# Full 128-column products in place of pairs of 64-column halves in a retention and MLP kernel

## The chip, the cores and the metric

The kernel runs on one core of one Trainium2 chip. The metric is device time in microseconds (us) of one execution; the median of three runs is compared.

## The reference

The first half is a retention layer: attention without softmax, with a decay that depends on the distance. Its output, brought to 4608 tokens of 512 values, goes through an MLP of 512 to 2048 to 512 with an exact GELU.

```python
# batch, heads, seq, head_dim = 8, 8, 576, 64
scores = q @ k.transpose(0, 1, 3, 2) / sqrt(64)
gamma = 1 - 2.0 ** (-5 - arange(8))
rel = pos[:, None] - pos[None, :]
ret = scores * where(rel >= 0, gamma ** rel, 0)
x = (ret @ v).transpose(0, 2, 1, 3).reshape(4608, 512)
h = x @ w_in                                   # 512 -> 2048
out = (0.5 * h * (1 + erf(h / sqrt(2)))) @ w_out   # 2048 -> 512
```

## The kernel before

**Attention.** Each of the 8 sequences of 576 positions is cut into four chunks of 128 and one of 64, 40 chunks in all. For each chunk q and k are brought into head-by-position form (`turn`): the first nine chunks by TensorE transposes (L301), the rest by DMA transposes that SP issues (L291). Then come the scores (`scores`, L326), the mask on VectorE (`masked`, L337), the product within the chunk (`inner`, L362), the running state (`states`, L385) and the product with the state (`cross`, L418). `evacuate` (L430) scales the result and writes it as bf16 into the ring xT, the MLP's input.

**MLP.** Tokens are taken in nine blocks of 512. `mlp1_step` (L466) makes one 128-row piece hT of the hidden layer out of four products over the 512 inputs, and ScalarE applies the GELU into g (L471). The second matrix product is done in a form with seven block products in place of eight; sums of blocks of g are made on VectorE (`sum_g`, L503 to L506), and `fast_step` (L573) multiplies. The last two blocks use the same scheme for the first matrix too (`lean_step`, L707).

**Halves.** In this kernel each product of the MLP, and each TensorE transpose, is a pair of matmuls: both take the same moving operand, one computes the output's partitions 0 to 63, the other 64 to 127. Each has a stationary operand of 128 x 64. The attention products `inner` and `states` have that shape too, while `scores` and `cross` use 64 x 64. The profile writes the shape used of TensorE's array as 128*64, 64*64 or 128*128.

**Order.** The instruction order of every engine is fixed when the kernel is built. The kernel holds a small planner: `clock` is its estimate of TensorE's time, `free_at` of when a PSUM bank is free, and each operation adds an estimate. The main loop asks which attention step is due (a list `PLAN` of group sizes and due times) and fills the rest with MLP steps, in the order of the lists `stages`. `tiled(n)` notes the shape in use (0 is the whole array, 1 is 128 x 64, 2 is 64 x 64) and adds 0.115 to the estimate when it changes. `POOL_0` is the estimate of when GpSimd's queue of loads is free. None of these estimates is an instruction; they only decide the order.

**Loads.** q, k and v are read by DMAs that GpSimd issues (L218), into nine buffers each; a load waits until the chunk nine before it has been used. The output is stored by DMAs that SP issues.

Of the kernel before, what the change touches and what calls it, by code (L numbers as in the profile page):

```python
# [16 lines left out]
def kernel(  # L17
# [14 lines left out]
    nc = tc.nc  # L32
# [9 lines left out]
    C = 128  # L42
    N_DM = d_model // 128
    N_DF = d_ff // 128
# [17 lines left out]
    LOADS = "1 2 3 i i i 4 i o i i 5 i i 6 o 7 o 8 o o o o o"  # L62
    T_LEAD = 4
    TR_LEAD = 5
    POOL_0 = 2.0
    LAND_0 = (2.9, 4.0, 5.0)
    CLOCK_0 = 3.2
    PLAN = [(1, 16), (1, 5), (1, 110), (0, 103), (1, 60), (1, 26), (1, 55), (0, 6), (2, 1), (1, 91), (0, 61), (1, 28), (2, 40), (2, 20), (2, 1), (1, 0), (2, 71), (2, 10), (2, 70), (2, 91), (2, 119), (2, 73), (2, 129), (2, 147), (2, 76), (2, 178), (2, 111), (1, 155), (0, 0), (0, 0)]
# [19 lines left out]
    RING = N_RING * TOK_BLK  # L88
    xT = const_pool.tile([128, N_DM, RING], BF16, name="xT")
# [179 lines left out]
        free_at[tag] = 1e6  # L269
        return ps.tile(shape, dtype, tag=tag, name=name), tag  # L270

    mode = [1]
    HALVES = (slice(0, 64), slice(64, 128))

    def tiled(n):

        if mode[0] != n:
            clock[0] += 0.115
        mode[0] = n

    def turn(i, parts=(0, 1)):

        cs = chunks[i][3]
        qk = loaded[i][0]
        s = st[i]
        if "qkT" not in s:
            s["qkT"] = tr_pool.tile([128, 2, HP, 128], BF16, tag="qkT", name="qkT")
            s["turned"] = 0.0
        qkT = s["qkT"]
        if i >= N_PE_TR:  # L290
            nc.sync.dma_start(qkT.rearrange("p j hp s -> p (j hp) s")[:, :, :cs],  # L291
                              qk[:cs].rearrange("p j h d -> p (j h d)"), transpose=True)
            transfer(1, clock[0] + T_FIX, T_DMA * cs / C, T_TAIL, s, "turned")
            return
        tiled(1 if cs == C else 2)
        for j in parts:
            wait((land_q, land_k)[j][i] + 0.1)
            ps_, tag = bank([128, HP, 128], BF16, "qk_ps")
            for hp in range(HP):
                for e, sl in enumerate(HALVES):  # L300
                    nc.tensor.transpose(ps_[sl, hp, :cs], qk[:cs, j, 2 * hp + e, :], ident[:cs, :cs])  # L301
            clock[0] += 0.23 * cs / C
            if i >= N_FIRST or i == 0:
                nc.vector.tensor_copy(qkT[:, j, :, :cs], ps_[:, :, :cs])
                end = on_dve(clock[0] + SEEN, HP * cs, 2)
            else:
                nc.scalar.copy(qkT[:, j, :, :cs], ps_[:, :, :cs])
                end = on_act(clock[0] + SEEN, HP * cs)
            free_at[tag] = end + BACK
            s["turned"] = max(s["turned"], end + BACK)  # L310
# [145 lines left out]
    def mlp1_step(t, m, lo, hi):  # L456
        tok0 = t * TOK_BLK
        mlp_begun[0] = True
        wait(land_in[m * 128 // W_IN_COLS])
        wait(x_ready(tok0 + lo, tok0 + hi))  # L460
        tiled(1)
        hT, tag = bank([128, TOK_BLK], FP32, "hT")
        w, o = w_in_sb[m * 128 // W_IN_COLS], m * 128 % W_IN_COLS
        for cc in range(N_DM):
            for sl in HALVES:
                nc.tensor.matmul(hT[sl, :hi - lo], lhsT=w[:, cc, o + sl.start:o + sl.stop],  # L466
                                 rhs=xT[:, cc, tok0 % RING + lo:tok0 % RING + hi],
                                 start=(cc == 0), stop=(cc == N_DM - 1), skip_group_check=True)
        clock[0] += N_DM * ((hi - lo) / 2400 + 0.0028)
        g_tile(t, m // 4)  # L470
        nc.scalar.activation(g_of(t, m, lo, hi), hT[:, :hi - lo], AF.Gelu)  # L471
        end = on_act(clock[0] + SEEN, hi - lo)
        free_at[tag] = end + BACK
        g_done(t, m, lo, hi, end + BACK)
# [36 lines left out]
    def left(t, which, j, p):  # L511

        if which[0] == "A":
            half, c = int(which[1]) - 1, int(which[2]) - 1
            lo = half * HALF + p * 128
            return g_of(t, 2 * j + c, lo, lo + 128)
        return s_tiles[t, j // 2][:, int(which[1]) - 1, j % 2, p * 128:(p + 1) * 128]

    def right(which, j):
        if which[0] == "B":  # L520
            c = int(which[2]) - 1
            return w_out_sb[:, j, int(which[1]) - 1, c * COL:(c + 1) * COL]
        return w_sum[:, int(which[1]) - 1, j]
# [30 lines left out]
    def fast_step(t, n):  # L554

        k, p = (LAST_ORDER if t == N_BLK - 1 else FAST_ORDER)[n]
        lhs, rhs, where = PRODUCTS[k]
        apart = t == N_BLK - 1
        f = fast.setdefault(t, {"end": {}})
        end = f["end"]  # L560
        pp = p if apart else 0
        key = (where, pp)
        wait(fast_ready(t, n))
        tiled(1)
        if k in (1, 2, 7) and (p == 0 or apart):
            if key in f:
                free_at[f[key][1]] = end["c11", pp]
            f[key] = bank([128, 2, COL], FP32, "fast")
        acc_ = f[key][0]
        fresh = k in (1, 2, 7)  # L570
        for j in range(N_DF // 2):
            for sl in HALVES:
                nc.tensor.matmul(acc_[sl, p, :], lhsT=left(t, lhs, j, p)[:, sl], rhs=right(rhs, j),  # L573
                                 start=(fresh and j == 0 and (p == 0 or apart)), stop=(j == N_DF // 2 - 1),
                                 skip_group_check=True)
        clock[0] += 0.1092 * (N_DF // 2)
        if p == 0 and not apart:
            return

        sl = slice(p, p + 1) if apart else slice(0, 2)  # L580
        width = COL if apart else 2 * COL
        ready = clock[0] + SEEN

        def buf(name, cols=COL):
            if name not in f:
                f[name] = o_pool.tile([128, 2, cols], FP32, tag=name, name=name, bufs=2 if name[0] == "o" else 1)
            return f[name]

        def psum(where):
            return f[where, pp][0][:, sl, :]  # L590

        def copy(dst, name, where):
            nc.scalar.copy(dst, psum(where))  # L593
            end[name, pp] = on_act(ready, width) + BACK

        def add(dst, name, where, to, after):
            nc.vector.tensor_tensor(dst, psum(where), f[to][:, sl], op=ALU.add)  # L597
            end[name, pp] = on_dve(max(ready, end[after, pp]), width) + BACK

        def store(half, c):  # L600
            row = t * TOK_BLK + half * HALF
            dst = out[row:row + HALF, :].rearrange("(p i) d -> i p d", p=2)
            src = f[f"o_sb{half}"]
            if apart:
                nc.sync.dma_start(dst[:, sl, c * COL:(c + 1) * COL], src[:, sl, c * COL:(c + 1) * COL])
            else:
                nc.sync.dma_start(dst, src)
                transfer(1, clock[0] + 3.0, 1.3, 2.0, f, "stored")

        if k == 1:  # L610
            copy(buf("m1")[:, sl], "m1", "P")
        elif k == 2:
            add(buf("o_sb0", d_model)[:, sl, :COL], "c11", "Q", "m1", "m1")
            if apart:
                store(0, 0)
        elif k == 6:
            copy(buf("u2")[:, sl], "u2", "P")
        elif k == 5:
            copy(buf("u4")[:, sl], "u4", "P")
        if k == (5 if apart else 7):  # L620
            add(buf("o_sb1", d_model)[:, sl, COL:], "c22", "Q", "u4", "u4")
            if apart:
                store(1, 1)
        if k == 3:
            copy(buf("o_sb0", d_model)[:, sl, COL:], "c12", "P")
            free_at[f["P", pp][1]] = end["c12", pp]
            store(0, 1)
        elif k == 4:
            add(buf("o_sb1", d_model)[:, sl, :COL], "c21", "Q", "u2", "u2")
            free_at[f["Q", pp][1]] = end["c21", pp]  # L630
            store(1, 0)
# [53 lines left out]
    def lean_step(t, n, x):  # L685
# [2 lines left out]
        lhs, rhs, where = PRODUCTS[k]  # L688
        f = lean.setdefault((t, n), {"end": {}})
        end = f["end"]  # L690
        tiled(1)
        if k in (1, 2, 7):
            if where in f:
                free_at[f[where][1]] = end["c11"]
# [2 lines left out]
        for p in range(2):  # L697
            j = 2 * n + p
            for cc in range(2):
                if lhs[0] == "A":  # L700
                    r, c = int(lhs[1]), int(lhs[2])
                    left_ = w_in_sb[j][:, 2 * (c - 1) + cc, (r - 1) * 128:r * 128]
                else:
                    left_ = w_in_sums[j][:, int(lhs[1]) - 1, cc]
                right_ = x_part(t, int(rhs[1]), int(rhs[2]))[:, cc] if rhs[0] == "B" else x_sums[t][int(rhs[1]) - 1][:, cc]
                for sl in HALVES:
                    nc.tensor.matmul(acc_[sl, p, :], lhsT=left_[:, sl], rhs=right_,  # L707
                                     start=(k in (1, 2, 7) and cc == 0 and p == 0), stop=(cc == 1), skip_group_check=True)
        clock[0] += 4 * 0.1092
        ready = clock[0] + SEEN  # L710

# [315 lines left out]
```

## Time and profile before

| | |
|---|---|
| median of 3 runs | 309.36 us (308.14 to 311.11) |
| the profiled execution: time, span | 311.11 us, 309.3 us |
| mean granted TensorE clock | 0.982 |
| TensorE products (PE) | 287.3 us busy, 93%, 5,353 matmuls |
| TensorE weight loads (PEld) | 238.8 us, 77%, 5,353 |
| VectorE (DVE) | 218.5 us, 71% |
| ScalarE (ACT) | 139.5 us, 45% |
| GpSimd (POOL) | 111.9 us, 36% |
| DMA | 35.91 MB in 153,620 packets |

The span runs from the first to the last instruction; the time has some more around it. The page cuts the span into 40 slices of 7.7 us. A matmul consists of two instructions, a weight load (LDWEIGHTS, listed under PEld) and a product (MATMUL, listed under PE). "Issue" is time in which an engine waited for nothing that the profile shows. In the listings by shape, `128*64 128x256` is a product with 128 rows and 64 columns of the array and 256 moving columns.

### The profile page before, as it was taken

What the parts mean: (1) busy time and instruction counts of PE and PEld (TensorE: products, weight loads), DVE (VectorE), ACT (ScalarE), POOL (GpSimd) and SP (SyncE); (2) the same over time, 40 slices, a digit from 0 to 9 for tenths busy, and PEclk for the clock granted to TensorE, in tenths of its full rate; (3) what the DMA queues carried; (4) which work ended last, traced back from release to release, by engine and by line L of the source; (5) the groups of instructions that cost most, each with busy time, mean ns of one, the idle gap of its engine ahead of it and who ended that gap; (6) DMA issues with size and microseconds to landing.
All of it is one profiled execution on the core that took longest, in us unless ns stands there. A gap on an engine that the chain in (4) does not pass through costs nothing.

```text
span 309.3 us, 11987 instructions
## 1 busy us (share of the span) xinstructions
PE 287.3 (93%) x5353; PEld 238.8 (77%) x5353; DVE 218.5 (71%) x488; ACT 139.5 (45%) x291; POOL 111.9 (36%) x139
## 2 busy tenths in 40 slices
PE   6999987997779977999999999999999999999995
PEld 2577686887769765975798569857975799999994
DVE  7765989438506784679918991898778777996452
ACT  4665564511414540227513651465145638687221
POOL 8978868647516305633842735000000000000000
PEclk9999999999989995999999999999999999999999
DMA  9999999999999999999999999560021000300033
GB/s 106 150 185 179 172 194 148 123 153 168 132 176 117 176 130 144 111 155 196 139 145 116 200 152 109 139 155 2 4 95 44 0 5 2 115 24 3 32 142 104
DMA packets 153620, 35.91 MB, mean 116 GB/s; under 512 B 142304, under 2 KB 149472, under 8 KB 153568
## 3 DMA queue, kind: packets, MB, share of 16 engines
q0 software_dynamic: 117872, 18.23, 94.6%
q1 hardware_dynamic: 35696, 16.91, 30.2%
q8 instruction: 42, 0.69, 1.0%
q14 instruction: 10, 0.08, 0.1%
HBM read 36.70 MB, written 9.44 MB: 149 GB/s over the span
## 4 chain that ended last, share of the span: by engine, by line
PE 87%; DVE 7%; issue 5%; DVEq 0%
PE fast L573 37%; PE hT L466 30%; PE lean L707 7%; PE sc L326 4%; PE o_ps L362 3%; PE o_ps L418 2%; PE qk_ps L301 1%; PE warm L890 1%; PE u_ps L385 1%; DVE ret L337 1%; DVE u L722 1%; DVE s L504 1%; DVE xT L430 1%; DVE s L506 0%; DVE s L503 0%
## 5 line engine op out<-in xcount | busy, mean ns | idle before, releaser
L466 PE MATMUL hT<-xT,w_in 128*64 128x512 bf16 (+6 forms) x1320 | 102.7, 311 | 4.4 <-issue 3.3
L471 ACT ACTIVATE g<-hT 128x512 bf16<-128x512 f32 (+6 forms) x165 | 73.8, 460 | 56.5 <-PE hT L466 54.7
L466 PEld LDWEIGHTS <-w_in 128*64 128x64 bf16 x1320 | 64.1, 110 | 36.3 <-issue 4.7
L573 PEld LDWEIGHTS <-s 128*64 128x64 bf16 x1152 | 64.5, 113 | 4.3 <-issue 3.2
L218 POOL DMA_DIRECT2D qk_ld<-in_q_dram x39 | 33.5, 859 | 59.2 <-DMA qkT<-qk_ld 32.2
L573 PE MATMUL fast<-w_sum,s 128*64 128x256 bf16 x864 | 51.3, 277 | 2.6 <-issue 2.6
L573 PEld LDWEIGHTS <-g 128*64 128x64 bf16 x864 | 47.8, 113 | 7.7 <-issue 6.0
L337 DVE TENSOR_TENSOR ret<-sc,msk 128x512 bf16<-128x512 f32 x64 | 40.9, 682 | 2.2 <-PE sc L326 2.1
L573 PE MATMUL fast<-w_out,g 128*64 128x256 bf16 x576 | 36.4, 284 | 3.3 <-issue 3.2
L597 DVE TENSOR_TENSOR o_sb<-fast,u 128x512 f32<-128x512 f32 (+1 forms) x20 | 12.7, 633 | 35.3 <-PE fast L573 29.2
L218 POOL DMA_DIRECT2D qk_ld<-in_k_dram x39 | 33.6, 861 | 8.0 <-DMA v_ld<-in_v_dram 6.8
L218 POOL DMA_DIRECT2D v_ld<-in_v_dram x39 | 33.7, 864 | 6.0 <-DVE s L506 1.2
L593 ACT COPY u<-fast 128x512 f32<-128x512 f32 (+1 forms) x20 | 10.9, 543 | 42.5 <-PE fast L573 42.5
L430 DVE TENSOR_TENSOR xT<-o_ps,dq 128x512 bf16<-128x512 f32 (+1 forms) x42 | 23.9, 604 | 0.3 <-PE o_ps L418 0.3
L347 DVE TENSOR_TENSOR vh<-v_ld,dv 128x512 bf16<-128x512 bf16 x32 | 21.2, 679 | 1.1 <-DMA v_ld<-in_v_dram 1.1
L573 PE MATMUL fast<-w_sum,g 128*64 128x256 bf16 x288 | 17.6, 274 | 1.8 <-issue 1.8
L503 DVE TENSOR_TENSOR s<-g 128x512 bf16<-128x512 bf16 x36 | 15.0, 418 | 5.3 <-ACT g L471 5.0
L573 PE MATMUL fast<-w_out,s 128*64 128x256 bf16 x288 | 18.6, 283 | 0.0
L400 ACT CAST u_sb<-run_sum 128x256 bf16<-128x256 f32 x24 | 9.7, 405 | 16.0 <-DVE run_sum L397 12.6
L504 DVE TENSOR_TENSOR s<-s,g 128x512 bf16<-128x512 bf16 x36 | 15.3, 425 | 1.2
L326 PE MATMUL sc<-qkT 64*64 64x128 bf16 (+1 forms) x576 | 13.8, 220 | 1.4 <-issue 1.3
L505 DVE TENSOR_TENSOR s<-g 128x512 bf16<-128x512 bf16 x36 | 15.1, 418 | 0.0
(82 smaller groups left out, 307.5 us busy)
## 6 DMA issues: line engine op xcount, KB each, us to landing
out_dram<-o_sb SPq DMA_DIRECT2D x16, 512.0 KB, 3.9
qk_ld<-in_k_dram POOLq DMA_DIRECT2D x32, 128.0 KB, 7.7
v_ld<-in_v_dram POOLq DMA_DIRECT2D x32, 128.0 KB, 7.9
qk_ld<-in_q_dram POOLq DMA_DIRECT2D x31, 128.0 KB, 7.7
w_in<-in_moe_w_in_dram POOLq DMA_DIRECT2D x8, 256.0 KB, 7.2
w_out<-in_moe_w_out_dram POOLq DMA_DIRECT2D x8, 256.0 KB, 7.9
out_dram<-o_sb SPq DMA_DIRECT2D x8, 128.0 KB, 2.4
qk_ld<-in_q_dram POOLq DMA_DIRECT2D x8, 64.0 KB, 6.8
```

What stands on the lines that cost most here:

```text
L218: nc.gpsimd.dma_start(dst[:cs], src[b, :, c0:c0 + cs, :].rearrange("h s d -> s h d"))
L326: nc.tensor.matmul(sc[e][lo:lo + 64, hp, :cs], lhsT=qkT[sl, 1, hp, lo:lo + 64], rhs=qkT[sl, 0, hp, :cs], start=True, stop=True, skip_group ...
L337: nc.vector.tensor_tensor(r[:cs, :, :cs], sc[e][:cs, :, :cs], msk[:cs, :, :cs].to_broadcast([cs, HP, cs]), op=ALU.mult)
L347: nc.vector.tensor_tensor(vh[:cs], loaded[i][1][:cs], dv[:cs, :, ci:ci + 1].to_broadcast([cs, H, D]), op=ALU.mult)
L430: nc.vector.tensor_tensor(xT[:, :, at:at + hi - lo], s["o_ps"][:, :, lo:hi], dq[:, :, c0 + lo:c0 + hi], op=ALU.mult)
L466: nc.tensor.matmul(hT[sl, :hi - lo], lhsT=w[:, cc, o + sl.start:o + sl.stop], rhs=xT[:, cc, tok0 % RING + lo:tok0 % RING + hi], start=(cc ...
L471: nc.scalar.activation(g_of(t, m, lo, hi), hT[:, :hi - lo], AF.Gelu)
L503: nc.vector.tensor_tensor(u[:, 0], a[2, 1], a[2, 2], op=ALU.add)
L504: nc.vector.tensor_tensor(u[:, 1], u[:, 0], a[1, 1], op=ALU.subtract)
L505: nc.vector.tensor_tensor(u[:, 2], a[1, 1], a[2, 1], op=ALU.subtract)
L573: nc.tensor.matmul(acc_[sl, p, :], lhsT=left(t, lhs, j, p)[:, sl], rhs=right(rhs, j), start=(fresh and j == 0 and (p == 0 or apart)), stop ...
L707: nc.tensor.matmul(acc_[sl, p, :], lhsT=left_[:, sl], rhs=right_, start=(k in (1, 2, 7) and cc == 0 and p == 0), stop=(cc == 1), skip_grou ...
```

## The change

The two halves of each MLP product and of each transpose become one product over the whole array, with a stationary operand of 128 x 128. The planner notes shape 0 for them. Its start value `POOL_0` goes from 2.0 to 2.2. The attention products are not changed. The change goes by the name of an index row made by a prefix scan on VectorE, with identity, mask and positions from it and no constants on GpSimd; these lines are the same in both kernels.

```diff
-    POOL_0 = 2.0
+    POOL_0 = 2.2
...
-    mode = [1]
-    HALVES = (slice(0, 64), slice(64, 128))
+    mode = [0]
...                                             # turn
-        tiled(1 if cs == C else 2)
+        tiled(0)
...
-                for e, sl in enumerate(HALVES):
-                    nc.tensor.transpose(ps_[sl, hp, :cs], qk[:cs, j, 2 * hp + e, :], ident[:cs, :cs])
+                nc.tensor.transpose(ps_[:, hp, :cs], qk[:cs, j, 2 * hp:2 * hp + 2, :], ident[:cs, :cs])
...                                             # mlp1_step
-        tiled(1)
+        tiled(0)
...
-            for sl in HALVES:
-                nc.tensor.matmul(hT[sl, :hi - lo], lhsT=w[:, cc, o + sl.start:o + sl.stop],
-                                 rhs=xT[:, cc, tok0 % RING + lo:tok0 % RING + hi],
-                                 start=(cc == 0), stop=(cc == N_DM - 1), skip_group_check=True)
+            nc.tensor.matmul(hT[:, :hi - lo], lhsT=w[:, cc, o:o + 128], rhs=xT[:, cc, tok0 % RING + lo:tok0 % RING + hi],
+                             start=(cc == 0), stop=(cc == N_DM - 1))
...                                             # fast_step
-        tiled(1)
+        tiled(0)
...
-            for sl in HALVES:
-                nc.tensor.matmul(acc_[sl, p, :], lhsT=left(t, lhs, j, p)[:, sl], rhs=right(rhs, j),
-                                 start=(fresh and j == 0 and (p == 0 or apart)), stop=(j == N_DF // 2 - 1),
-                                 skip_group_check=True)
+            nc.tensor.matmul(acc_[:, p, :], lhsT=left(t, lhs, j, p), rhs=right(rhs, j),
+                             start=(fresh and j == 0 and (p == 0 or apart)), stop=(j == N_DF // 2 - 1),
+                             skip_group_check=True)
...                                             # lean_step: the same
```

More of the change, by code (lines that the diff above doesn't have):

```diff
@@ L690, in lean_step @@
         end = f["end"]
-        tiled(1)
+        tiled(0)
         if k in (1, 2, 7):
@@ L705, in lean_step @@
                 right_ = x_part(t, int(rhs[1]), int(rhs[2]))[:, cc] if rhs[0] == "B" else x_sums[t][int(rhs[1]) - 1][:, cc]
-                for sl in HALVES:
-                    nc.tensor.matmul(acc_[sl, p, :], lhsT=left_[:, sl], rhs=right_,
-                                     start=(k in (1, 2, 7) and cc == 0 and p == 0), stop=(cc == 1), skip_group_check=True)
+                nc.tensor.matmul(acc_[:, p, :], lhsT=left_, rhs=right_, start=(k in (1, 2, 7) and cc == 0 and p == 0),
+                                 stop=(cc == 1), skip_group_check=True)
         clock[0] += 4 * 0.1092
```

## The prediction

> **What bounds the kernel now.** I read the page first, then the waits of TensorE, the table of stretches, the instructions by shape, the timeline around a change of tile, and the built order of both kernels. TensorE (PE) is busy 93% of the span and carries 87% of the chain that ended last. What holds it up is in the chain's "issue 5%": time in which it waited for nothing that the profile shows.
>
> ```profile
> PE 87%; DVE 7%; issue 5%; DVEq 0%
> PEclk9999999999989995999999999999999999999999
> q8 instruction: 42, 0.69, 1.0%
> ```
>
> The clock row has two dips, in the slices at about 93 and 120 us. Now the waits of PE between 43 and 125 us, all of them:
>
> ```profile
> PE fast L573 <- issue: 7.7, 4, 3.2
> PE hT L466 <- issue: 3.3, 3, 1.6
> PE sc L326 <- issue: 1.3, 2, 0.9
> PE o_ps L362 <- DVE ret L337: 0.7, 2, 0.4
> PE o_ps L418 <- issue: 0.3, 1, 0.3
> ```
>
> The issue rows add up to 12.6 us in ten stops; only 0.7 us is a wait for data. I cut the span exactly at these stops and counted matmuls between them (columns: length, PE busy, matmuls, granted clock, DMA share, GB/s):
>
> ```profile
> 51.82:66.95 15.13, 14.54 (x256) 1.00 2.43 133
> 66.95:73.97 7.02, 5.19 (x128) 1.00 1.99 133
> 73.97:81.53 7.56, 5.95 (x128) 1.00 2.35 170
> 81.53:89.38 7.85, 5.67 (x128) 1.00 2.44 172
> 96.12:102.04 5.92, 5.46 (x128) 1.00 1.42 159
> 109.33:118.27 8.94, 5.75 (x128) 0.96 1.74 112
> ```
>
> Every stop comes after 128 matmuls or a multiple, whatever they compute. A matmul is two instructions, a weight load and a product, so that is 256 instructions. The instruction queue moved 42 packets, 0.69 MB, 16.4 KB each; PE's built order has 10,706 such instructions, 42 times 255. So PE stops because its next packet of instructions is not there. When stops follow each other, the time from one to the next is how long a packet takes to come: 7.02, 7.56, 7.85, 6.74, 5.92, 7.29, 8.94 us, on average 7.3, with the DMA engines loaded. After 125 us such stops are absent.
>
> The stops cost twice. Behind the longest two (2.2 us before 89.4, 3.2 us before 118.3) the granted clock was halved:
>
> ```profile
> 90.20:93.60 3.40, 3.40 (x38) 2.94 (x34) 0.69 (x1) 0.58 (x1) 0.00 (x0) 0.50 2.07 133
> 117.50:124.30 6.80, 6.02 (x58) 5.00 (x60) 2.16 (x6) 0.59 (x1) 2.48 (x3) 0.50 1.99 165
> ```
>
> That is 10.2 us at half speed, 5.1 us lost.
>
> **The change, part by part.** The diff touches only TensorE's products and the planner's notes on tiling. The index row, identity and mask that the change's name speaks of stand in both kernels, and POOL issues the same DMAs in the same order: nothing. POOL_0 is a planner's estimate. In the built orders the products, their widths and SP's list are the same; two things move: in the first 18 us some warm-up products and transposes, and at 107 us one attention group comes one hT step (8 of the old matmuls at 82 ns, 0.65 us) earlier. I cost both at nothing: the start waits for loads (PE's first transposes wait 1.6 us for a cast of q), and the transposed chunk needed at 107 us landed 4.1 us before its use. Without that cover the second costs at most 0.65 us.
>
> *Instructions.* 3,928 pair halves become 1,964 full products, so 10,706 instructions become 6,778, 26 packets for 42. Between 43 and 125 us the products are 1,031 of the MLP, 16 of transposes and 356 of attention, which stay: 1,403 become 880. Without stops and half clock the 82 us hold 82 - 12.6 - 5.1 = 64.3 us of work. A packet of 128 products therefore lasts 64.3 x 128 / 1403 = 5.9 us now, less than the 7.3 us that one takes to come, and 64.3 x 128 / 880 = 9.4 us then, more. Gain: 12.6 + 5.1 = 17.7 us if no packet is late. Laying the old times along the new order, all packets in this stretch last 7.8 us or more except two between 94 and 109 us, rich in attention, with 6.3 and 7.3 us. Against the mean of 7.3 they lose 1.0 us, against the longest of 8.9 they lose 4.3. I take 1.5 us back, bounds 0 and 6.
>
> *Stream time.* Pairs of 256 columns start 109 ns apart, of 512 columns 216, of 128 columns 56 (192 matmuls of line 573 take 10.58 us in the chain at 152 us, 110 ns a pair). Time follows the columns, so the stream sets it and both halves run at once; one full product streams the same columns. Fewer weight loads gain nothing here, since they are not the bound: lower bound 0. The only full-width products of this trace are the warm-up's, 512 columns at half clock, whose starts lie 427 ns apart, twice 213: their loads are hidden. Whether that holds at 128 to 256 columns and full clock no row shows. The upper bound comes from the half loads:
>
> ```profile
> L573 PEld LDWEIGHTS <-s 128*64 128x64 bf16 x1152 | 64.5, 113 | 4.3 <-issue 3.2
> L152 PEld LDWEIGHTS <-zeros 128*128 128x128 bf16 x6 | 0.7, 136 | 2.3 <-DVE ones L119 1.2 <-issue 1.1
> ```
>
> 64.5 us for 1,152 is 56 ns a half, 112 for both. If a full load took 112 and bound, the 1,284 products of 256 columns would lose 3 ns each (3.6 us), the 136 of 128 columns 56 (7.6), the 72 of 192 columns 29 (2.1), the 8 of 64 columns 80 (0.6), the 72 transposes 56 (4.0): 17.9 us. I take 0, because the full load's record is of the same length as a half's (96 ns at full clock against 110) and the warm-up hides it; the 17.9 goes to a rival.
>
> The Trainium skill ("TensorE: Matmul & The Clock Gate", LDWEIGHTS) speaks against the change: a load takes its columns divided by 1.2 in ns, 107 ns for 128 columns. By that, an estimate, the widths of 64 to 192 columns would lose some 9 us and the sum would end near 308. The same page (weight-path modes) and "TensorEngine Tiling (Array Packing)" say that a fast load exists for 128 columns of bf16 and that column tiling excludes it; by that nothing is lost. No run here shows which.
>
> *Changes of tile.* Here is one attention group, with the starts in the first column:
>
> ```profile
> 167.62 0.38 PE L466 MATMUL hT<-xT,w_in 128*64 128x512 bf16 x2
> 167.84 0.42 PE L385 MATMUL u_ps<-vh,qk_ld 128*64 128x64 bf16 x16
> 168.09 0.62 PE L362 MATMUL o_ps<-ret,vh 128*64 128x128 bf16 x16
> 168.64 0.64 PE L326 MATMUL sc<-qkT 64*64 64x128 bf16 x32
> 169.11 0.39 PE L418 MATMUL o_ps<-qkT,u_sb 64*64 64x128 bf16 x8
> 169.43 2.85 PE L466 MATMUL hT<-xT,w_in 128*64 128x512 bf16 x24
> ```
>
> hT to u_ps keeps the tile 128*64: a pair of 512 takes 0.216 us and u_ps starts 0.22 later. o_ps to sc changes it: 16 products at 28 ns end at 168.54, sc starts at 168.64. The last row does so again: 169.11 + 8 x 28 ns = 169.33, hT at 169.43. So 0.10 us a change. With full products the step from the MLP into u_ps or o_ps is a change too. The new order has 21 of these, 18 of them after 43 us, all on PE: 1.8 us. Earlier ones lie under the loads.
>
> *What is late next.* With PE 17 us earlier at 125 us, others may be late. The tightest is at 118 us: the four quads of s (L503 to L506) run on DVE from 112.47 to 119.01, and the products with s come 64 matmuls (3.5 us) after 113.73, so at 117.2 in place of 122.6; the sums they need end near 118.4. That is 1.2 us. Transposes landed 4.1 to 26 us before their scores in this stretch. SP issues them after PE's own steps, so they move with it, and where the margin is under 6 us the stops between issue and use are under 1 us. I take 2.0 us for such waits in all, bounds 0 and 5.
>
> The sum on the profiled execution: span 309.3 - 17.7 + 1.5 + 1.8 + 2.0 = 296.9, plus the 1.8 us that its time of 311.11 has around the span: 298.7. The median shown, 309.36, is 1.75 lower than that execution; I read that as fewer late packets, which the new kernel has few of either way, so I don't subtract it again.
>
> **The rivals.**
> *Packets are still late in half the cases.* For: the same bytes must pass in 64 us, so 7.3 us may become 7.3 x 82 / 64 = 9.4, just the new packet's length. Against: the longest turn measured is 8.9. Half the stops and half the lost clock come back: 298.7 - 1.5 + 8.9 = 306.
> *The stretch is bound by its transfers.* For: the DMA share is at its top until 205 us. Then the gain is eaten and the changes of tile remain: median plus 1.8, 311. Against: no PE row waits for a DMA, and POOL's loads wait 22.0 us for u_ps products (L385), so they follow PE.
> *The full weight load binds.* 298.7 + 17.9 = 317. It turns the result when the 1,892 MLP products lose 7 ns each on average (13.8 us). For: the trace has no full products back to back at full clock. Against: the warm-up's.
> *The change does not do what it says* holds for the index row and GpSimd, priced at 0.
>
> **How the numbers follow.** My forecast (near 299) has 0.65, late packets 0.15, transfers 0.08, the weight load 0.12. About 1% can be told from no change in this kernel. So faster 0.80, same 0.08, slower 0.12. Predicted is 298.7. The forecast's own bounds are 298.7 - 3.5 = 295 and 298.7 + 7.5 = 306; the runs before spread by 3 us, which takes the low end to 293, and late packets in half the cases need 308 above. What lies outside, transfers and the weight load, is 0.20.
>
> **What would show it.** Between 43 and 125 us the issue rows of PE should fall from 12.6 us to under 3, the instruction packets from 42 to about 27, the clock dips vanish, the fast products of 256 columns keep 109 ns each, and a start 0.10 us late should appear before each u_ps group. If products of 128 columns are over 80 ns apart, the weight load was mis-costed; if issue rows of 6 us or more remain, the packet's turn was; if DVE or DMA rows take their place, the waits were.

## The result, and the profile after

The changed kernel takes 294.88 us (median of 4 runs) against 310.24 us for the kernel before (4 runs); the ratio is 0.949, with a 95% interval of 0.940 to 0.958. One of the four runs after, of 299.8 us, was in a slower state with a lower clock and is left out of the ratio. The profiled execution took 294.92 us, its span is 293.2 us.

The page of the kernel after, the rows that answer to those shown of before: chain by engine, granted clock, instruction queue.

```profile
PE 47%; DMA 38%; DVE 10%; issue 2%; POOL 2%; POOLq 0%; DVEq 0%
PEclk9999999999999999999999999999999999999999
q8 instruction: 26, 0.43, 0.7%
```

The two dips of the clock are gone, and 26 packets of instructions came in place of 42. The chain now runs through the loads for a good part; below I test whether that means they bound the kernel.

The waits of PE between 42 and 125 us, the stretch that had 12.6 us of issue rows:

```profile
PE o_ps L360 <- DVE ret L335: 0.7, 2, 0.4
PE hT L463 <- issue: 0.5, 1, 0.5
```

One stop is left, 0.5 us, at 97.1 us: it ends the second of the two packets rich in attention that the prediction named, the one of 7.3 us.

The DMA records in the traces show these packets themselves, so the cause need not rest on the count of instructions. In the kernel before, each of the ten stops ended 1.3 to 1.6 us after a packet of 16,384 bytes of the instruction queue had landed: packets landed at 72.68, 80.04 and 87.81 us, and PE went on at 73.98, 81.54 and 89.39. The one stop of the kernel after ended 1.5 us after such a landing, at 95.62 us. Every other packet of that kernel between 36 and 202 us landed at least 2.1 us before its first product, by the count of 128 products a packet.

Three pieces of the same stretch (length, then busy time and instructions of PE, PEld, DVE, ACT and POOL, then clock, DMA share and GB/s):

```profile
57.90:66.00 8.10, 8.10 (x81) 7.06 (x80) 2.76 (x6) 1.56 (x3) 5.44 (x7) 1.00 2.05 153
82.00:90.00 8.00, 8.00 (x163) 6.86 (x164) 6.15 (x12) 3.60 (x10) 4.48 (x7) 1.00 1.82 212
90.00:98.00 8.00, 7.45 (x128) 5.42 (x125) 7.41 (x15) 4.15 (x10) 3.65 (x5) 1.00 1.80 132
```

PE is busy nearly all the time, with 81 to 163 matmuls in 8 us, so a packet of 128 lasts 6 to 13 us, and 163 is the exception. The DMA share and rate are about as high as before: 1.95 and 166 GB/s from 42 to 106.5 us, against 2.00 and 149 from 43 to 125 us.

Whether a full product costs more than a pair is best read from the end of the two chains, a long row of products of 256 columns without attention. The first line is of the kernel before, the second of the kernel after:

```profile
285.63 20.10 PE fast L573 x368
```

```profile
269.96 20.10 PE fast L568 x184
```

368 halves and 184 full products take the same 20.10 us, 109 ns a pair or a product. Full products of 512 columns start 216 ns apart, and those of 128 columns 56 ns, as the pairs did. In the kernel after (timeline; start, length, line, products) the 28 products of 128 columns take 1.57 us from the first start to the next row's:

```profile
99.83 1.73 PE L463 MATMUL hT<-xT,w_in 128*128 128x128 bf16 x28
101.40 3.66 PE L568 MATMUL fast<-w_out,g 128*128 128x256 bf16 x32
```

The start of an attention group in the kernel after, in the same columns:

```profile
150.63 0.38 PE L463 MATMUL hT<-xT,w_in 128*128 128x512 bf16 x1
150.94 0.44 PE L383 MATMUL u_ps<-vh,qk_ld 128*64 128x64 bf16 x16
```

The last hT product starts at 150.63 and streams for 0.216 us, to 150.85; u_ps starts at 150.94. Before, it followed without a pause: this is the added change of tile, 0.09 us.

Laid side by side at the start of the same scores, the gain builds up and shrinks: chunk 17 at 125.0 before and 106.5 after (18.5 us ahead), chunk 39 at 231.1 and 215.5 (15.6), the end at 309.3 and 293.2 (16.1).

### The profile page after: what moved, and what is told of

The parts are those of the page before. It is cut to its first block, busy times and chain, and to the rows that moved or that the text cites. A ratio compares the mean times of both kernels' runs of the same rounds, so it can differ in the third digit from the quotient of the medians.

```text
span 293.2 us, 8058 instructions
## 1 busy us (share of the span) xinstructions
PE 282.0 (96%) x3389; PEld 211.6 (72%) x3389; DVE 218.3 (74%) x488; ACT 139.5 (48%) x291; POOL 112.0 (38%) x139
## 4 chain that ended last, share of the span: by engine, by line
PE 47%; DMA 38%; DVE 10%; issue 2%; POOL 2%; POOLq 0%; DVEq 0%
PE fast L568 19%; DMA qk_ld<-in_k_dram 18%; PE hT L463 14%; DMA v_ld<-in_v_dram 14%; PE lean L701 8%; DMA qk_ld<-in_q_dram 6%; DVE ret L335 2%; PE sc L324 1%; PE o_ps L360 1%; DVE xT L428 1%; POOL qk_ld L218 1%; PE qk_ps L299 1%; PE warm L884 1%; DVE s L500 1%; PE u_ps L383 1%
## 5 line engine op out<-in xcount | busy, mean ns | idle before, releaser
L463 PE MATMUL hT<-xT,w_in 128*128 128x512 bf16 (+6 forms) x660 | 102.0, 311 | 1.3 <-DVE xT L428 0.7
L463 PEld LDWEIGHTS <-w_in 128*128 128x128 bf16 x660 | 56.1, 98 | 40.2 <-DVE xT L428 1.5
L568 PEld LDWEIGHTS <-s 128*128 128x128 bf16 x576 | 55.8, 98 | 9.3 <-DVE s L500 2.5
L568 PE MATMUL fast<-w_sum,s 128*128 128x256 bf16 x432 | 49.5, 273 | 1.8 <-DVE s L500 1.7
L568 PEld LDWEIGHTS <-g 128*128 128x128 bf16 x432 | 41.6, 98 | 5.7
L568 PE MATMUL fast<-w_out,g 128*128 128x256 bf16 x288 | 33.6, 273 | 0.0
L568 PE MATMUL fast<-w_out,s 128*128 128x256 bf16 x144 | 17.3, 272 | 0.0
L568 PE MATMUL fast<-w_sum,g 128*128 128x256 bf16 x144 | 17.3, 273 | 0.0
L502 DVE TENSOR_TENSOR s<-g,s 128x512 bf16<-128x512 bf16 x36 | 15.0, 418 | 0.0
```

Source lines behind the costliest of these rows:

```text
L463: nc.tensor.matmul(hT[:, :hi - lo], lhsT=w[:, cc, o:o + 128], rhs=xT[:, cc, tok0 % RING + lo:tok0 % RING + hi], start=(cc == 0), stop=(cc ...
L502: nc.vector.tensor_tensor(u[:, 3], a[1, 2], u[:, 1], op=ALU.subtract)
L568: nc.tensor.matmul(acc_[:, p, :], lhsT=left(t, lhs, j, p), rhs=right(rhs, j), start=(fresh and j == 0 and (p == 0 or apart)), stop=(j == N ...
```

## The experiments

The theory is that the gain comes from the number of instructions alone: PE's packets arrive too late while the DMA engines are loaded. The main rival is that the full shape is cheaper in itself.

**Full shape, twice the instructions.** Each MLP product issued from 41 to 109 us is cut along its moving columns; `whole()` is false in that stretch of the planner's clock.

```diff
+    whole = lambda: not 38.0 <= clock[0] < 106.0
+    def product(out_, lhsT, rhs, start, stop):
+        if whole(): ...                     # one matmul, as after
+        n = rhs.shape[-1] // 2
+        for c, sl in enumerate((slice(0, n), slice(n, 2 * n))):
+            nc.tensor.matmul(out_[:, sl], lhsT=lhsT, rhs=rhs[:, sl], start=start and c == 0, stop=stop, ...)
```

> The kernel after, but each MLP product issued between 41 and 109 us is cut in two along its moving columns: same 128*128 shape of the array, same stationary operand in both, same changes of tile, but twice the instructions in that stretch (548 more products, each with its load). Theory (instructions arrive too late): the stops after each 256 instructions come back, 8 to 13 us of issue rows on PE between 43 and 125 us, with one or two dips of the clock; with 548 x 2.5 ns = 1.4 us for the second starts the time is 304 to 314 us. Rival (the full shape itself is cheaper, the number of instructions does not matter): 295 + 1.4 = 296 us, no stops.

Measured: 309.62 us, 0.994 of the kernel before (0.988 to 0.9985). The shape, the stationary operands and the changes of tile are those of the kernel after, and the gain is gone. Its waits of PE from 43 to 125 us, and the matmuls between four stops (length, PE busy, matmuls, clock, DMA share, GB/s):

```profile
PE o_ps L372 <- issue: 4.5, 2, 2.5
PE fast L283 <- issue: 4.0, 3, 2.1
PE hT L283 <- issue: 3.5, 3, 1.7
PE sc L336 <- issue: 1.2, 1, 1.2
```

```profile
62.19:70.02 7.83, 6.67 (x128) 1.00 2.06 154
70.02:78.13 8.11, 6.06 (x128) 1.00 1.66 154
78.13:85.15 7.02, 6.06 (x128) 0.76 2.27 171
85.15:93.81 8.66, 6.62 (x128) 1.00 1.85 167
```

These are 13.2 us of stops, again 128 matmuls apart, and there are three dips of the clock of 3.4 us each. All nine stops ended 1.3 to 1.9 us after a packet had landed. This profiled execution was 1.2% above the median, so its stops are somewhat more than the median's. The rival would have given 296.

**Pairs of halves in that stretch only.**

```diff
-        n = rhs.shape[-1] // 2 ...
+        for sl in HALVES:
+            nc.tensor.matmul(out_[sl], lhsT=lhsT[:, sl], rhs=rhs, start=start, stop=stop, ...)
...
-        tiled(0)
+        tiled(0 if whole() else 1)
```

> The kernel after, with the pairs of 64-column halves of before only for the MLP products issued between 41 and 109 us, and full products elsewhere. Theory: nearly all of the loss returns, since all stops of before lay there: 306 to 312 us, issue rows of 8 to 13 us. Rival (the full shape is cheaper everywhere): only the share of this stretch in the MLP's products returns, 548 of 1892, 29% of 15 us: 299 us.

Measured: 307.7 us, 0.989 of before (0.985 to 0.993), inside the theory's range; its profile, of an execution 2% above that median, has 15.9 us of issue rows, more than the 8 to 13 expected. So 29% of the products carry most of the difference.

**Pairs of halves after that stretch only** (`whole` is `clock[0] < 106.0`).

> The complement: full products until 109 us, pairs of halves from there on. Theory: no stop late, as before had none after 125 us, and the 12 changes of tile between the MLP and u_ps or o_ps after 109 us are saved: 294.9 - 1.2 = 293.7 us. Rival (the full shape is cheaper everywhere): 71% of 15 us returns, 305 us.

Measured: 301.38 us, 0.971 of before (0.966 to 0.975). Both expectations missed, the theory's by 7.7 us and the rival's by 3.6. The profiled execution took 303.34 us. Its waits of PE after 109 us, then a stretch between two stops and two dips:

```profile
PE o_ps L370 <- issue: 3.1, 2, 2.9
PE fast L282 <- issue: 2.3, 1, 2.3
```

```profile
114.77:123.16 8.39, 5.52 (x128) 0.96 2.41 173
122.50:129.30 6.80, 6.13 (x68) 0.50 1.62 165
156.60:160.00 3.40, 3.40 (x26) 0.50 1.44 214
```

5.4 us of stops and 5.1 us of lost clock, in work where the kernel before had none. So the absence of stops after 125 us in the kernel before was not a property of that work: at the same place in the program, but earlier in time, packets came late again. Why they did so here and not in the kernel before is not shown. I had read a quiet stretch of one run as a safe one.

**Pairs of halves at the end only**, after the loads have landed (`whole` is `clock[0] < 198.0`), beside the kernel after once more.

> The kernel after, with pairs of halves for the 696 MLP products after 202 us, when the loads and the DMA transposes have landed. Theory (a packet is late only while the DMA engines are loaded): no stop there, three changes of tile fewer, so within 1 us of the kernel after, 294 to 296 us. Rival (late halves cost by themselves, which could also be read from the late halves' 301.4): 696 of the 1,208 late products, 58% of 6.5 us, 3.8 us more: 298.7 us.

> The kernel after once more, unchanged, as the measure for the three others on the same chip: 293 to 297 us, at most 1 us of issue rows on PE.

Measured: 295.4 us with the late pairs, 296.09 without, 0.956 of before for both (intervals 0.948 to 0.964 and 0.950 to 0.963). No issue row is left after 202 us. From the scores of chunk 39 to the end the profiled executions take 77.9 us with pairs and 77.6 us without, so the 3.8 us by which the rival came to 298.7 are not there. Three changes of tile fewer are too little to see.

**Fewer DMA packets under the kernel before.** First only the loads:

```diff
-            nc.gpsimd.dma_start(dst[:cs], src[b, :, c0:c0 + cs, :].rearrange("h s d -> s h d"))
+            nc.gpsimd.dma_start(dst[:cs], src[b].rearrange("h s d -> (h s d)")[c0 * d_model:(c0 + cs) * d_model]
+                                .rearrange("(p h d) -> p h d", h=H, d=D))
```

> The kernel before, all halves and all 10,706 instructions of PE kept; from chunk 1 on, q, k and v are read as contiguous runs of 512 values per partition in place of eight rows of 64 from eight heads (the same bytes into the same buffers, so the values are those of other heads and positions): an eighth of the packets of the loads. Theory (packets of instructions are late because the DMA engines are loaded): the turn falls below 5.9 us, stops mostly go, 294 to 300 us. Rival (the stops belong to the number of instructions whatever the DMAs do, or the gain came from the shape): 307 to 311 us, with the stops or without them.

Measured: 300.46 us, 0.971 of before (0.965 to 0.977). That is 0.5 us above the theory's range and well under the rival's. 153,620 DMA packets became 59,540. The waits of PE from 40 to 125 us that are issue rows:

```profile
PE fast L574 <- issue: 5.2, 4, 2.2
PE hT L467 <- issue: 2.4, 2, 1.6
```

In the profiled execution (299.41 us, against 311.11 before) the issue rows fell from 12.6 to 7.6 us, the two dips of the clock are gone, which is 5.1 us, and 1.0 us is gained up to 37 us. That makes 11.1 of 11.7 us. The other three executions have mean clocks of 0.987 to 0.994, so they had dips. The stops did become fewer, but they did not mostly go. Then the DMA transposes too, in both kernels, which leaves 37,652 packets:

```diff
-            nc.sync.dma_start(qkT.rearrange("p j hp s -> p (j hp) s")[:, :, :cs], ..., transpose=True)
+            if cs == C:
+                nc.sync.dma_start(qkT.rearrange("p j hp s -> p (j hp s)"), qk.rearrange("p j h d -> p (j h d)"))
+            else: ...                       # as before
```

> The kernel before with the contiguous loads of the earlier run and, besides, the DMA transposes of the 128-row chunks replaced by plain DMA copies of the same bytes (the values in qkT are not transposed; the short chunks keep theirs): few packets in both queues, the same 10,706 instructions of PE. Theory: the turn of a packet falls clearly below 5.9 us, the issue rows fall from 7.6 us to under 2, no clock dip, 291 to 295 us. Rival (a packet of instructions is late whatever the load): 299 to 301 us as with the contiguous loads alone.

> The kernel after with the same two edits of its loads and transposes. Theory: it has no late packets to lose, so it stays at 292 to 295 us, and against the kernel before with the same edits it is 1 to 2 us slower, by its 18 changes of tile of 0.10 us. Rival (full products are cheaper in themselves): 10 us or more faster than the kernel before with these edits. Second rival (transfers bound the kernel after): it falls under 290 us.

Measured: 292.19 us with pairs of halves (ratio to before 0.943, 0.938 to 0.948), 291.12 us with full products (0.941, 0.935 to 0.947). The waits of PE from 40 to 125 us in the kernel with halves and light transfers:

```profile
PE o_ps L366 <- DVE ret L341: 0.7, 2, 0.4
PE fast L577 <- issue: 0.6, 1, 0.6
PE hT L470 <- issue: 0.6, 1, 0.6
```

With all its 10,706 instructions the kernel of halves runs within 1.1 us of the other once most of its packets come in time; 1.2 us of stops are still in it. So the full products are not cheaper in themselves, or by no more than that. I had expected the halves to win by 1 to 2 us. The 1.2 us of stops and 0.5 us at the start (at 36 us the kernel of full products is ahead by that much) explain that they do not win. That they lose by 0.5 us between the profiled executions (291.57 and 291.11), and by 1.1 between the medians, is not explained. The kernel after gains 5.0 us from light transfers (296.09 - 291.12). So the transfers do cost it something, more than I had allowed (292 at least), though not the 6 us and more by which the second rival came under 290.

**Earlier transposes in the kernel after** (`TR_LEAD` 7 in place of 5), beside the unchanged kernel.

> The kernel after with the DMA transposes issued up to seven chunks ahead of the scores in place of five. In the kernel after the tightest one landed 0.2 us before its scores, and in its second profiled run the scores waited 1.7 us for one, with a dip of the clock behind it. Theory (with the stops gone, the next thing late are the DMA transposes): waits of scores for qkT at 0, no dip, 1 to 3 us less than the unchanged kernel of this call, 292 to 295 us. Rival (the margin is enough in most runs; an earlier transpose only moves the queue of loads): within 1 us of the unchanged kernel.

> The kernel after, unchanged, on the same chip as the measure for the run with earlier transposes: 294 to 297 us, with the scores waiting up to 2 us for a transpose.

Measured: 294.31 and 294.24 us. No time came of the earlier transposes: the rival holds. In the profile PE had no wait for qkT, but the unchanged kernel had none this time either, against the up to 2 us expected of it, so the profiles do not show what the edit would save where there is one. PE waited 2.3 us for the sums s, with a dip of 3.4 us; in the unchanged kernel it waited 2.8 us for them, without a dip.

## Why the prediction was right

*The stops.* Named as late packets of 256 instructions, 12.6 us, and 5.1 us of halved clock. They fell to 0.5 us and none. Doubling the instructions alone brought them back, thinning the DMA packets alone took nearly all of them away, in two steps (12.6, 7.6 and 1.2 us), and the packets' landings stand in the traces; both halves of the mechanism are shown. Given back for late packets were 1.5 us; 0.5 was measured. The longer turn of the rival did not come: the one stop left is where the walk along the new order had put it.

*Stream time.* Priced at 0, and the two chains agree to 0.01 us in 20.1. The rival of the weight load (317 us) is out. The Trainium skill ("TensorE: Matmul & The Clock Gate", LDWEIGHTS) would have 107 ns for a load of 128 columns. The row of the full loads in the kernel after:

```profile
L568 PEld LDWEIGHTS <-s 128*128 128x128 bf16 x576 | 55.8, 98 | 9.3 <-DVE s L500 2.5
```

They are listed with 98 ns each, yet products of 128 columns, each with its load, start 56 ns apart, and those of 64 columns in the run with twice the instructions 29 ns. So the load binds nothing here. What the skill says of the fast load fits that, but no run shows which kind of load these are.

*Changes of tile.* 0.10 us each, 18 after 43 us: measured 0.09, and the trace has the 18. From chunk 17 to chunk 39 the new kernel loses 2.9 us: 11 changes more, 1.1 us, and two waits for the sums s, 1.7 us.

*What is late next.* 2.0 us taken, 1.7 measured as waits on s, but not where I put it and not for the reason I gave, so the near agreement is luck. I named the block whose sums ended at 119 us before; that one had no wait in the first profile. The waits came in the two following blocks. The timeline shows why for the first:

```profile
136.37 0.69 DVE L345 TENSOR_TENSOR vh<-v_ld,dv 128x512 bf16<-128x512 bf16 x1 [2.02 <-DMA v_ld<-in_v_dram]
136.98 0.42 DVE L499 TENSOR_TENSOR s<-g 128x512 bf16<-128x512 bf16 x1
139.38 1.81 PE L568 MATMUL fast<-w_sum,s 128*128 128x256 bf16 x15 [1.05 <-DVE s L500]
```

VectorE stood 2.0 us before a scaling of v that waited for its load, with the sums queued behind it. Before the second wait it stood 3.3 us for another load of v. I had looked for a late VectorE; it was a late transfer. In repeats of the same kernel the next late thing was another: a transpose (1.7 us, with a dip) in the second, the sums (2.8 us) in the third. I read this as the margin that the stops had given the transfers; with light transfers the waits for s come to 0.2 us.

*The size.* 298.7 was 3.8 us too high. The terms: late packets 1.0 and waits 0.3 less than taken; 0.7 us at the start, which I had priced at nothing and where the new kernel is ahead at 37 us (36.52 against 37.18); 0.5 us after chunk 39; and 1.3 us in the stretch of the stops that no wait row holds, which I can't place. For the start, fewer changes of tile between warm-up products and transposes are a possible reason; that was not tried by itself.

*The rival of the transfers* had something in it: they no longer hide behind the stops. The 5.0 us that light transfers give the kernel after are the most that it can be in these runs, as the light transfers also take away the stop of 0.5 us.

## What to carry to other kernels

Count instructions between unexplained stops: if the number is the same every time, whatever the instructions do, the engine may be waiting for its program, and the landings of the instruction queue's packets in the DMA records tell whether it is. The remedy is fewer instructions for each microsecond of work, or fewer DMA packets beside it (shown here for the time alone: the kernels with light transfers compute other values); two matmuls that run at once halve the time that a packet of instructions lasts, though they cost the array nothing. A stretch without stops is no proof of safety when its neighbours will move.

## What the runs showed of the hardware

A packet of 256 PE instructions took 5.9 to 8.9 us to come with the DMA engines loaded, from the end of one stop to the end of the next. Its own transfer took 0.9 to 2.1 us, and PE went on 1.3 to 1.6 us after it had landed; the rest passed before the transfer began. With a quarter of the DMA packets only two stops of 0.6 us were left in the kernel of halves, where a packet lasts 5.9 us on average, so most came within that.

The clock's dip does not follow from the length of one stop. Stops of 2.2 and 3.2 us had one at their end in the kernel before, and so had a wait of 1.7 us in the second profile of the kernel after. Stops of 2.9 us in the kernel with early halves and of 2.2 us in the one with contiguous loads had none, and neither had two waits of 1.7 and 1.1 us close together in the third profile of the kernel after. Every dip between the kernel's start and its end lasted 3.4 us or twice that.
